# Spatial-bias buffer allocated and cleared in the opening step; ORDER and WAYS tables replaced

## The chip, the cores and the metric

The kernel runs on one core of one Trainium2 chip. The metric is device time in microseconds (us) of one execution. A core has TensorE (PE, with its weight loads shown as PEld), VectorE (DVE), ScalarE (ACT) and GpSimd (POOL). SyncE (SP) issues DMAs here and computes nothing. ACT and POOL issue DMAs as well. Each engine takes its instructions strictly in the order in which the program emits them.

## The reference, cut to what matters

Three blocks follow one another: block-causal attention, a mixture of four attention experts with two chosen per token, and a gated MLP with a spatial mix.

```python
B, H, S, D = 8, 8, 576, 64
a = softmax(mask_blocks(q @ k.T / 8)) @ v                # block-causal, blocks of 64
x = a.transpose(0, 2, 1, 3).reshape(B, S, 512)
top2, w = gate(x @ w_gate)                               # 2 of 4 experts per token
x = sum(w_e * (causal_attention(x @ wq[e], x @ wk[e], x @ wv[e]) @ wo[e]) for e in top2)
h = relu(x @ w_in)                                       # 512 -> 1024
u, v = h[..., :512], h[..., 512:]
v_s = w_spatial @ layernorm(v) + b_spatial[:, None]      # mixes the 576 positions
out = (u * v_s) @ w_out
```

## The kernel before

**Work.** The kernel goes through the 8 batches. A batch has four pairs of heads of the first attention, keys (b,0) to (b,3), and two pairs of experts, keys (b,4) and (b,5). For a pair, the steps are: `lq` and `lv` load q, k and v into a `nat` tile; `mg` finds their largest magnitude; `pq` and `pv` split q, k and v into two f16 numbers each; `sc` makes scores, their maxima and exponentials in four parts; `w` (function `weights`) splits the exponentials into two f16 numbers, a cast (first piece) and a subtraction (second piece); `wt` transposes them by a DMA from SP; `av` multiplies them with v; `x` (function `halves`) normalizes and transposes the result. For a batch, the dense steps follow: `begin`, `proj`, `vproj`, `gate`, `hv`, `norm`, `gu`, `gs`, `outp`.

**Weights.** In the first 200 us the weights are prepared beside batch 0 and 1, by the `su` steps. `ldA` loads wq, wk, wv and the gate weights. `ldB` loads w_spatial in six DMAs and then the bias b_spatial in three one-row DMAs (L615). The bias lands in a part of the tile `wspb` (`t["b"]`, 576 columns) that is set to zero first by a VectorE memset (L611). That memset stands in the seventh of the nine pieces of `ldB`. `max` takes the largest magnitudes (L632), `scale` makes scales from them, then come `cons`, `split`, `wsp` (transposes of w_spatial) and `win`, `wm`, `wout`, `wf1` to `wf3` (products of wo and w_in, and w_out).

**Order.** Every step is cut into pieces of one engine each. The list `ORDER` names the step whose next piece is emitted, so it fixes the place of each piece on each engine's queue. It was written by a planner that isn't part of the kernel. The table `WAYS` says which engine does a piece that more than one could do: A is ACT, D is DVE, G is POOL, S is SP. An entry such as "w.2.0" lists the ways for pair 2, part 0, batch by batch; the last one holds for all later batches. In "AD" the first letter is the cast and the second the subtraction. The planner's costs (`sua("ldB", ...)`, L1512) count the DMAs of `ldB`, and not the memset.

**Around the bias.** On SP, the queue in the order before runs: `ldB` pieces 1 to 6, piece 7 (the first bias DMA, after the memset), `wt` (0,0).2, `wt` (0,0).0, `ldB` 8 and 9, then `wt` (0,1).0 to 2. On DVE, the memset has 64 pieces of other steps ahead of it. On PE, `av` (0,0) comes directly ahead of the transpose of `max` (L200) and of `pq` (0,3).

Of the kernel before, what the change touches and what calls it, by code (L numbers as in the profile page):

```python
# [10 lines left out]
F32 = mybir.dt.float32  # L11
# [12 lines left out]
P = 128  # L24
# [12 lines left out]
def attn_moe_gmlp_kernel(  # L37
# [17 lines left out]
    V, A, G, T = nc.vector, nc.scalar, nc.gpsimd, nc.tensor  # L55
# [454 lines left out]
    def startup():  # L510
# [59 lines left out]
        def s_open():  # L570
            opened("su")
            TILES["x64"] = wf16.rearrange("p t c m -> p (t c m)").bitcast(U16).rearrange("p (n s) -> p n s", n=2)
# [4 lines left out]
        def s_ldA(way):  # L577
# [15 lines left out]
            t["sa"] = su.tile([P, NC], F32, name="wsa")  # L593
            V.memset(t["sa"], 0.0)

        def s_ldB(way):
# [3 lines left out]
            wb = t["wb"] = su.tile([P, 2048], F32, name="wspb")  # L600
# [9 lines left out]
            t["b"] = wb[:, 1280:1280 + S]  # L610
            V.memset(t["b"], 0.0)  # L611
# [152 lines left out]
    def dense(b, keep):  # L764
# [831 lines left out]
```

## Time and profile before

| | us |
|---|---|
| median of 3 runs | 959.12 (958.43 to 960.29) |
| the profiled execution | 963.83 |
| its span, first to last instruction | 962.10 |
| PE busy in the span | 842.6 (88%) |
| DVE busy | 734.7 (76%) |
| ACT busy | 640.0 (67%) |
| POOL busy | 533.2 (55%) |

The time of the profiled execution is 1.73 us above its span and 4.71 us above the median. The views below give busy times by stretch, waits by their releaser (the instruction whose end let the waiting one go), and the instructions in order of time. In the order of time, a bracket such as [1.73 <-DMA pT<-p] is the idle time of that engine before the instruction and what ended it.

### The profile page before, as it was taken

What the parts mean: (1) busy time and instruction counts of PE and PEld (TensorE: products, weight loads), DVE (VectorE), ACT (ScalarE), POOL (GpSimd) and SP (SyncE); (2) the same over time, 40 slices, a digit from 0 to 9 for tenths busy, and PEclk for the clock granted to TensorE, in tenths of its full rate; (3) what the DMA queues carried; (4) which work ended last, traced back from release to release, by engine and by line L of the source; (5) the groups of instructions that cost most, each with busy time, mean ns of one, the idle gap of its engine ahead of it and who ended that gap; (6) DMA issues with size and microseconds to landing.
All of it is one profiled execution on the core that took longest, in us unless ns stands there. A gap on an engine that the chain in (4) does not pass through costs nothing.

```text
span 962.1 us, 25183 instructions
## 1 busy us (share of the span) xinstructions
PE 842.6 (88%) x10038; PEld 615.3 (64%) x10038; DVE 734.7 (76%) x1602; ACT 640.0 (67%) x1159; POOL 533.2 (55%) x529
## 2 busy tenths in 40 slices
PE   3646778678999899989899999999999999999987
PEld 1444657556776677656676777666766776567654
DVE  5879979978879867887687889676898776568361
ACT  1664756987578758786577879675877767637232
POOL 6426335764673778767366667654457755516300
PEclk9777899789999999999999999999999999999999
DMA  9689988998889788999399978996799929932701
GB/s 201 161 154 213 203 164 138 179 173 142 148 161 200 126 154 149 187 184 173 75 154 214 143 145 178 160 176 121 149 172 193 153 48 160 185 70 47 157 8 55
DMA packets 472844, 143.66 MB, mean 149 GB/s; under 512 B 458307, under 2 KB 464771, under 8 KB 472726
## 3 DMA queue, kind: packets, MB, share of 16 engines
q1 hardware_dynamic: 464166, 130.31, 75.3%
q0 software_dynamic: 4944, 10.85, 4.9%
q8 instruction: 79, 1.29, 0.6%
q10 hardware_dynamic: 3616, 0.89, 0.5%
q14 instruction: 39, 0.32, 0.1%
HBM read 38.19 MB, written 9.44 MB: 50 GB/s over the span
## 4 chain that ended last, share of the span: by engine, by line
PE 53%; DVE 12%; DMA 5%; ACT 4%; issue 3%; SPq 2%; POOL 1%; DVEq 0%; ACTq 0%; POOLq 0%
PE duo L803 8%; PE duo L470 8%; PE duo L979 8%; PE duo L997 7%; PE duo L882 5%; PE duo L826 4%; PE duo L393 4%; DMA pT<-p 4%; PE duo L963 3%; DVE st L414 3%; PE duo L408 2%; ACT pf L435 2%; PE duo L345 2%; DVE qk L239 1%; DVE pf L499 1%
## 5 line engine op out<-in xcount | busy, mean ns | idle before, releaser
L455 POOL TENSOR_TENSOR p<-pf,p 128x512 f16<-128x512 f32 (+1 forms) x200 | 244.3, 1246 | 89.1 <-ACT p L352 34.1
L414 DVE TENSOR_REDUCE st<-duo 128x2 f32<-128x1024 f32 (+2 forms) x192 | 151.1, 814 | 31.2 <-PE duo L403 19.6
L470 PEld LDWEIGHTS <-pT 128*128 128x128 f16 x4320 | 143.0, 99 | 39.4 <-DMA pT<-p 21.8
L393 PE MATMUL duo<-qk 64*128 64x256 f16 (+3 forms) x1152 | 110.7, 313 | 19.7 <-DVE qk L239 11.7
L435 ACT ACTIVATE pf<-duo,st,es 128x512 f32<-128x512 f32 (+2 forms) x224 | 122.5, 615 | 8.2 <-DVE st L426 4.2
L356 POOL TENSOR_SCALAR p<-pf 128x1024 f16<-128x1024 f32 (+1 forms) x61 | 68.3, 1122 | 92.0 <-issue 26.7
L470 PE MATMUL duo<-v,pT 128*128 128x65 f16 (+1 forms) x2880 | 100.4, 195 | 20.0 <-DMA pT<-p 14.7
L979 PE MATMUL duo<-wsp,vn 128*128 128x288 f16 x832 | 111.6, 286 | 1.4 <-DVE vn L928 0.7
L803 PE MATMUL duo<-x,wqk 128*128 128x288 f16 x768 | 102.8, 294 | 6.8 <-DVE neh L218 3.9
L979 PEld LDWEIGHTS <-vn 128*128 128x128 f16 x832 | 80.1, 98 | 23.0 <-DVE vn L928 1.7
L803 PEld LDWEIGHTS <-wqk 128*128 128x128 f16 x768 | 76.3, 100 | 28.7 <-issue 6.9
L997 PE MATMUL duo<-wo,gT 128*128 128x512 f16 x384 | 85.7, 379 | 0.0
L393 PEld LDWEIGHTS <-qk 64*128 64x128 f16 x1152 | 46.4, 98 | 53.7 <-issue 36.4
L435 ACT ACTIVATE pf<-duo,st,mt 128x256 f32<-128x256 f32 (+3 forms) x128 | 69.9, 618 | 5.2 <-DVE st L426 2.5
L504 POOL TENSOR_TENSOR xh<-pf,xh 128x640 f16<-128x640 f32 x33 | 47.0, 1424 | 37.2 <-ACT xh L352 23.3
L997 PEld LDWEIGHTS <-gT 128*128 128x128 f16 x384 | 36.7, 98 | 42.7 <-DVE gT L986 0.5
L352 ACT CAST p<-pf 128x1024 f16<-128x1024 f32 (+1 forms) x59 | 62.7, 1064 | 0.7
L451 DVE TENSOR_TENSOR p<-pf,p 128x1024 f16<-128x1024 f32 (+1 forms) x44 | 57.4, 1305 | 7.3 <-POOL p L356 3.9
L470 PE MATMUL duo<-V,pT 128*128 128x65 f16 (+1 forms) x1440 | 50.3, 195 | 8.9 <-DMA pT<-p 5.5
L345 PE MATMUL duo<-ident,nat 128*128 128x128 f32 x320 | 51.3, 291 | 7.6 <-ACT pf L435 4.0
L826 PE MATMUL duo<-wvg,x 128*128 128x260 f16 x480 | 56.7, 274 | 1.3 <-ACT pf L435 0.9
L882 PE MATMUL duo<-wf,x 128*128 128x512 f16 x240 | 54.4, 379 | 0.6 <-DMA x<-xh 0.6
(273 smaller groups left out, 1681.5 us busy)
## 6 DMA issues: line engine op xcount, KB each, us to landing
out_dram<-pf SPq DMA_DIRECT2D x16, 512.0 KB, 4.4
nat<-in_q_dram SPq DMA_DIRECT2D x42, 128.0 KB, 3.1
nat<-in_k_dram SPq DMA_DIRECT2D x42, 128.0 KB, 3.3
wf<-in_moe_w_in_dram SPq DMA_DIRECT2D x8, 512.0 KB, 5.5
nat<-in_v_dram SPq DMA_DIRECT2D x32, 128.0 KB, 2.9
nat<-in_v_dram POOLq DMA_DIRECT2D x30, 128.0 KB, 5.7
nat<-in_q_dram POOLq DMA_DIRECT2D x20, 128.0 KB, 4.1
nat<-in_k_dram POOLq DMA_DIRECT2D x20, 128.0 KB, 4.6
```

The source lines that it names most:

```text
L345: T.transpose(ps[:, P * c:P * c + r], p.nat[0:r, i, c, :], ident[0:r, 0:r])
L356: G.tensor_scalar(hi, src, 1.0, 1.0, op0=OP.mult, op1=OP.mult)
L393: T.matmul(ph[:, hh, o:o + w], p.q[hs, a, ts], p.k[hs, bb, 0:w], start=i == 0, stop=False)
L414: V.reduce_max(st[:, 0, 2 * c:2 * c + 2], ph[:, :, off[c]:off[c] + P * (c + 1)], axis=AX.X)
L435: A.activation(pf[:, n * hh + off[c]:n * hh + off[c] + w], ph[:, hh, off[c]:off[c] + w], AF.Exp, bias=st[:, 1, 2 * c + hh:2 * c + hh + 1], ...
L455: G.tensor_sub(lo[:, z:z + m], src[:, z:z + m], hi[:, z:z + m])
L470: T.matmul(ps[:, hh, o:o + n], pT[:, col(t, kk):col(t, kk) + P], p.v[:, hh, kk, a:a + n], start=kk == 0 and i == 0, stop=kk == nk - 1 and ...
L803: T.matmul(ps[:, MID + a:MID + a + w], wqk16[:, l, c, 2 * n + i, :], x16[c][:, r, a:a + w], start=m == 0, stop=m == 11)
L826: T.matmul(ps[:, i, :260], x16[d][:, l, P * c:P * c + P], wvg16[:, r, d, :], start=m == 0, stop=m == 11)
L882: T.matmul(ps[:, i], h16[d][:, l, P * c:P * c + P], wf16[:, r, d, FH:], start=m == 0, stop=m == 5)
L979: T.matmul(ps[:, MID + a:MID + a + n], l, wsp16[:, r, c, a:a + n], start=i == 0, stop=i == 13)
L997: T.matmul(ps[:, i], gT[:, x, d, P * c:P * c + P], wo16[:, y, d, :], start=m == 0, stop=m == 11)
```

## The change

The step `open`, which only opened the pool of weight buffers, now also allocates `wsa` and `wspb` and clears both `wsa` (5 columns) and the bias part of `wspb` (576 columns), on VectorE. `ldA` and `ldB` no longer do so. Nothing else in the functions or in the planner's costs differs. `ORDER` and `WAYS` are replaced as a whole; the list has the same 3671 entries for the same 1366 steps.

```diff
         def s_open():
             opened("su")
+            t["sa"] = su.tile([P, NC], F32, name="wsa")
+            V.memset(t["sa"], 0.0)
+            t["wb"] = su.tile([P, 2048], F32, name="wspb")
+            t["b"] = t["wb"][:, 1280:1280 + S]
+            V.memset(t["b"], 0.0)
...
             t["st"] = su.tile([P, 5], F32, name="wst")
-            t["sa"] = su.tile([P, NC], F32, name="wsa")
-            V.memset(t["sa"], 0.0)
...
-            wb = t["wb"] = su.tile([P, 2048], F32, name="wspb")
+            wb = t["wb"]
...
-            t["b"] = wb[:, 1280:1280 + S]
-            V.memset(t["b"], 0.0)
             for i in range(3):
...
     ORDER = (
-        50, 54, 50, 54, 51, 50, 50, 50, 54, 50, 50, 52, 142, 142, 142, 143, 51, 62, 54, 143, 143, 0, 54, 143, 143,
-        54, 19, 143, 58, 58, 66, 54, 1, 58, 51, 66, 66, 56, 67, 67, 58, 58, 144, 67, 70, 1, 144, 144, 71, 62, 1, 58,
...
+        50, 54, 54, 51, 50, 50, 50, 50, 54, 50, 50, 52, 142, 142, 142, 143, 143, 51, 54, 54, 143, 54, 143, 62, 143,
+        143, 54, 66, 58, 51, 67, 56, 58, 66, 58, 58, 66, 67, 67, 144, 144, 70, 58, 70, 58, 62, 0, 58, 144, 62, 62, 1,
...
-        "lv.3": ("G", "G", "G", "S", "G", "S", "S", "G"), "mg.0.0": ("D", "D", "A", "D", "A", "A", "D", "A"),
-        "mg.1.1": ("A", "A", "D", "A", "A", "A", "A", "D"), "mg.2.0": ("D", "A", "A", "A", "A", "A", "A", "D"),
-        "mg.2.1": ("D", "D", "D", "D", "A", "D", "A", "D"), "mg.3.0": ("A", "A", "D", "D", "A", "D"),
-        "pv.1": ("A", "A", "D", "G", "A", "G", "D", "G"), "pv.2": ("A", "G", "G", "A", "D", "A", "D", "G"),
-        "w.0.2": ("GG", "DG", "DG", "GG", "GG", "DG", "GD", "AD"), "w.1.0": ("DG", "DG", "GG"),
-        "w.1.1": ("DG", "AG", "GG", "GG", "GG", "GG", "AG", "GG"), "w.1.2": ("DD", "GG", "DG", "GG", "DG", "GG"),
-        "w.2.0": ("AD", "GG", "DD", "AG", "DD", "AD", "AD", "AG"),
-        "w.2.2": ("DD", "AD", "GG", "GG", "GG", "AG", "AD", "AG"), "w.3.0": ("AD", "AG", "AD", "DD", "DG", "GG"),
...
+        "lv.3": ("G", "G", "G", "S", "S", "S", "G"), "mg.0.0": ("D", "A", "A", "D", "A"),
+        "mg.1.1": ("A", "A", "D", "A", "D", "A", "D", "A"), "mg.2.0": ("A", "A", "A", "A", "D", "A", "D", "A"),
+        "mg.2.1": ("A", "D", "D", "A", "D", "A", "D", "A"), "mg.3.0": ("A", "A", "D", "D", "A", "D", "A"),
+        "pv.1": ("A", "D", "A", "G", "G", "A", "A", "G"), "pv.2": ("A", "G", "G", "G", "G", "A"),
+        "w.1.0": ("AG", "DG", "GG", "GG", "GG", "GG", "AG", "GG"), "w.1.1": ("DG", "AG", "GG"),
+        "w.1.2": ("AD", "GG", "AG", "GG", "DG", "GG"), "w.2.0": ("GG", "GG", "AG", "GG", "AD", "AD", "GD", "GG"),
+        "w.2.2": ("GD", "AD", "GG", "AG", "AG", "AG", "DD", "GG"), "w.3.0": ("AD", "DG", "DD", "GG", "DG", "GG"),
...
```

With the step names put in for the numbers, the start of the new list reads as follows. On DVE, `open` comes after the maxima of `sc` (0,0).0, which are its 13th piece. On SP, `ldB` 1 to 4 are mixed with `ldA`; then come `ldA` 13, `win` 1, `wt` (0,0).1, `ldB` 5, `wt` (0,0).0, `ldB` 6 to 8 (with the first two bias DMAs), `wt` (0,0).2 and `ldB` 9. The load of `win` 0 is the 13th issue on SP, where it was the 8th. On ACT, the second piece of `win` 0 keeps its place ahead of the first exponentials. Of the 620 pieces on PE, 370 keep their place in PE's order, 188 move by one place, and none by more than six.

## Rows read from the trace of the kernel before

**Rows 1.** Busy time in stretches: us, then PE, PEld, DVE, ACT, POOL (x instructions), clock, DMA share, GB/s.
```profile
40.00:60.00 20.00, 6.74 (x66) 4.08 (x65) 17.13 (x36) 13.97 (x31) 6.61 (x6) 0.67 0.44 91
80.00:100.00 20.00, 14.28 (x95) 10.71 (x95) 18.81 (x30) 11.43 (x20) 11.72 (x18) 0.67 1.16 207
100.00:120.00 20.00, 15.76 (x188) 14.86 (x188) 18.82 (x36) 15.15 (x27) 8.60 (x6) 0.94 1.11 198
160.00:200.00 40.00, 27.43 (x424) 21.06 (x423) 39.09 (x78) 35.39 (x70) 29.14 (x31) 0.85 1.06 181
300.00:400.00 100.00, 93.14 (x1202) 69.37 (x1200) 79.32 (x172) 73.53 (x138) 72.83 (x71) 1.00 0.88 157
sum 962.00, PE 842.55 PEld 615.30 DVE 734.74 ACT 639.99 POOL 533.25; mean PE 44.34 PEld 32.38 DVE 38.67 ACT 33.68 POOL 28.07
```

**Rows 2.** Waits of SP's queue, whole span: waiter and releaser, total us, times, longest us.
```profile
SPq L615 <- DVE wspb L611: 15.2, 1, 15.2
```

**Rows 3.** Order of time, 34 to 65 us: start us, us, engine, line, operation [idle before <-releaser].
```profile
34.91 2.38 POOL L455 TENSOR_TENSOR p<-pf,p 128x544 f16<-128x544 f32 x2
...
35.99 0.48 SPq L608 DMA_DIRECT2D wspb<-in_moe_w_spatial_dram  x1
...
51.15 0.54 DVE L611 MEMSET wspb<- 128x576 f32 x1
...
52.13 4.56 SPq L460 DMA_TRANSPOSE pT<-p  x2
...
56.93 0.73 DVE L354 CAST p<-pf 128x1088 f16<-128x1088 f32 x1 [1.73 <-DMA pT<-p]
...
59.35 2.86 PE L470 MATMUL duo<-v,pT 128*128 128x65 f16 x49 [12.72 <-DMA pT<-p]
59.91 0.75 DVE L632 TENSOR_REDUCE wst<-wspb 128x1 f32<-128x576 f32 x1 [0.79 <-DMA wspb<-in_moe_b_spatial_dram]
...
64.49 0.17 DVE L486 TENSOR_SCALAR rr<-duo 128x10 f32<-128x10 f32 x1 [3.63 <-PE duo L470]
```

**Rows 4.** DVE's instructions by form: line, shapes, count, busy us, mean ns, idle before.
```profile
L297 DVE TENSOR_REDUCE mst<-nat 128x2 f32<-128x1280 f32 x14 | 20.7, 1477 | 6.3 <-DMA nat<-in_q_dram 3.8 <-DMA nat<-in_k_dram 2.4
L297 DVE TENSOR_REDUCE mst<-nat 128x1 f32<-128x640 f32 x15 | 11.9, 809 | 1.3 <-DMA nat<-in_v_dram 1.3
L354 DVE CAST p<-pf 128x1024 f16<-128x1024 f32 x17 | 11.6, 683 | 0.0
L354 DVE CAST p<-pf 128x1088 f16<-128x1088 f32 x7 | 5.3, 757 | 1.8 <-DMA pT<-p 1.7
L451 DVE TENSOR_TENSOR p<-pf,p 128x1024 f16<-128x1024 f32 x29 | 35.6, 1229 | 4.6 <-POOL p L356 3.9 <-ACT p L352 0.5
L426 DVE TENSOR_SCALAR st<-st,es 128x2 f32<-128x2 f32 x16 | 6.1, 382 | 0.4
```

**Rows 5.** The same view for ACT and POOL.
```profile
L295 ACT ACTIVATE junk<-nat 128x640 bf16<-128x640 f32 x53 | 38.9, 734 | 0.9
...
L455 POOL TENSOR_TENSOR p<-pf,p 128x512 f16<-128x512 f32 x134 | 164.0, 1248 | 46.9 <-DVE p L354 13.4 <-ACT p L352 11.6 <-DVE es L326 7.4
...
L356 POOL TENSOR_SCALAR p<-pf 128x1024 f16<-128x1024 f32 x40 | 45.3, 1133 | 59.7 <-ACT pf L435 25.5 <-issue 18.3 <-DVE eso L324 10.0
```

**Rows 6.** Instructions on `wspb`, L543: ns min/median/max; then the slowest in order of time.
```profile
L543 DVE SCALAR_TENSOR_TENSOR wspb<-wf,wspb x4: 691/693/1594, 87.6 to 116.3; 128x512 int32<-128x512 int32 x4
...
111.49 3.29 POOL L455 TENSOR_TENSOR p<-pf,p 128x544 f16<-128x544 f32 x2 [1.68 <-ACT p L352]
112.11 1.59 DVE L543 SCALAR_TENSOR_TENSOR wspb<-wf,wspb 128x512 int32<-128x512 int32 x1
```

**Rows 7.** Order of time at the start: the load of `win` 0 and its readers.
```profile
9.30 0.58 SPq L531 DMA_DIRECT2D wf<-in_moe_w_in_dram  x1
...
17.88 0.66 ACT L537 ACTIVATE x<-wf 128x512 f32<-128x512 f32 x1
...
24.34 1.93 ACT L435 ACTIVATE pf<-duo,st,eso 128x384 f32<-128x384 f32 x4
```

**Rows 8.** PE's waits from 200 to 950 us, the two largest: total us, times, longest.
```profile
PE duo L470 <- DMA pT<-p: 7.5, 6, 2.0
PE duo L393 <- DVE qk L239: 6.3, 8, 2.4
```

421 rows, old and new, of tables (ORDER, WAYS) are left out of this document.

## The prediction

> **What bounds the kernel now.** I read the busy times by stretch first. They split the run in two. In a stretch of the middle, 300 to 400 us, PE is busy 93.14 of 100 us: from there on PE's own work sets the pace. Ahead of 200 us it does not: from 40 to 60 us PE is busy 6.74 of 20 us, while DVE is busy 17.13; from 80 to 120 us DVE is busy 37.6 of 40 us, and from 160 to 200 us 39.09 of 40 [rows 1]. So the weights and the first batches are held by DVE, and what the change is worth is read there, from DVE's idle time and DVE's work. Over the whole span PE is idle 962 − 842.55 = 119 us [rows 1], which is the most that any order could take away.
>
> Then I read the waits of SP's queue. The first bias DMA (L615) waited 15.2 us for the memset (L611), once [rows 2]. The order of time shows it: SP issued its last w_spatial DMA at 35.99 us and was free at 36.47; DVE came to the memset only at 51.15 us, because 64 pieces of other steps lie ahead of it in its order. Behind the waiting DMA stand two transposes (L460) that went out at 52.13 us, though the POOL subtraction that made the later of their inputs ended at 34.91 + 2.38 = 37.29 us. PE, whose next work is `av` (0,0), stood idle for 12.72 us for them and started at 59.35 [rows 3].
>
> The 15.2 us are not the gain, and neither are PE's 12.72, since DVE worked on through nearly all of that time. What DVE itself lost by the wait is its idle time with a releaser behind the stalled queue: 1.73 us before a cast that needs a buffer which a transpose gives back, 0.79 us before the maximum of the bias, which had just landed, and 3.63 us before the first instruction after `av` (0,0). Together **6.15 us** [rows 3].
>
> **The change, part by part.**
>
> *The wait.* In the new order the memset is emitted after DVE's 13th piece, the maxima of the first score block, many pieces ahead of the place where SP first needs it. So the three bias DMAs find it done, and SP goes on. What is late next on SP is its own transposes: the one of `w` (0,0).2 needs data that POOL had at 37.29 us, against a queue free at 36.47 [rows 3]; a wait of about 1 us takes the place of 15.2. What is late next on DVE is DVE's own work: the maximum of the bias comes after it in any case. I take the whole 6.15 us. Ends: 0, if the same three idle times return with another releaser, and 6.15.
>
> *The memset itself* costs 0.54 us on DVE [rows 3] and is moved, not removed. It lay in a stretch where DVE was nearly full and goes to one that it shares with the first maxima. Zero; ends −0.6 to +0.6. The clearing of five columns that is moved with it is less than a tenth of a us of these.
>
> *The table: what DVE loses up to the step `begin` of batch 0.* Comparing the entries of the two tables for the pieces that both lists emit before it: `mg` (0,2) and (1,0), first parts, go to ACT, 2 × 1.477; `mg` (0,2), second part, 0.809; the casts of `w` (0,1).0 at 0.683 and of `w` (0,1).2 and `w` (0,2).2 at 0.757 each go to ACT and POOL; the subtraction of `w` (0,2).0 goes to POOL, 1.229 [rows 4]. Sum 7.19 us. To DVE come, net, two small instructions of `sc` at 0.382 and one cast of `pv` (1,1), which I price like the cast at 0.683: 1.45 us [rows 4]. So DVE has 5.74 us less to do. It is worth this only where DVE has no idle time: 80 to 120 and 160 to 200 us, 80 of the 160 us after 40 [rows 1]. I take half, **2.9 us**; ends 0 and 5.74. ACT gets three magnitudes in five instructions at 0.734 and two casts; in 40 to 60 us it was busy 13.97 of 20 [rows 1, 5], so I price that at nothing. If that cover is gone it costs what ACT gains, near 4 us.
>
> At this point a rule of the Trainium skill speaks against the new table. The trace first: four equal instructions of L543 took 0.69 us, and 1.59 us in the one case that ran beside POOL's subtraction, which itself took 3.29 us for two halves where two others of the same shape took 2.38 [rows 3, 6]. The Trainium skill, "SBUF — State Buffer", section "Who interferes with whom", says that VectorE and GpSimd share one pair of ports and that the later one blocks fully where a VectorE instruction has two SBUF inputs and the other reads SBUF. By it, each of the three pieces that POOL takes over in pair 2 here (both of `w` (0,2).0, the cast of `w` (0,2).2) would hold DVE for up to 1.59 − 0.69 = 0.90 us, 2.7 us in all, and the table's 2.9 would be 0.2. The trace agrees with the rule in this one pair of rows; how often the pairs will meet in the new order it cannot show.
>
> *The order at the start.* The load of `win` 0 becomes SP's 13th issue, where it was the 8th. It was issued at 9.30 us and read by ACT at 17.88, and the first exponentials behind it on ACT began at 24.34 [rows 7]. A load takes at most 17.88 − 9.30 = 8.6 us by these rows. Five issues later at 0.6 us (the row's own 0.58) is 12.3 us and lands by 20.9, ahead of 24.34: free. If the five issues take three times that, it lands at 26.9 and costs ACT 2.6 us. I take 1 us; ends 0 and 2.6.
>
> *The order later.* PE's order is nearly the same: 370 of 620 pieces keep their place and 188 move by one. So a gain made ahead of 200 us moves all later work forward. But each engine's queue is laid anew, and which small waits fall away or appear can't be told from the tables. PE's two largest waits after 200 us, 7.5 and 6.3 us in total [rows 8], bound it: half of these 13.8 us, about 7 us, either way. I take 0.
>
> *Sum.* −6.15 − 2.9 + 1 = −8.05 us. Against the profiled execution's own time, 963.83, this gives 955.8. The median of the runs is 4.71 below that execution, so I forecast 959.12 − 8.05 = **951 us**.
>
> **The rivals.**
>
> *The gain does not last (same).* DVE's idle time of 6.15 us returns elsewhere, and the lighter table is taken up by ACT or by DVE's clashes with POOL. For it: the DMA share is 1.16 and 1.11 in 80 to 120 us [rows 1], so transfers already stand in line there and earlier issues may only wait longer. Against it: the share is 0.44 in 40 to 60 us [rows 1], which is where the stalled transposes will now run. Time 959, chance 0.11.
>
> *POOL becomes the last link (slower).* Up to the outputs of batch 0 the new table gives POOL seven casts of `w` and takes one, at 1.133, and gives it two subtractions of two halves each, at 1.248 [rows 5]: 6 × 1.133 + 4 × 1.248 = 11.8 us; what it gives and takes of `pv`, `x` and `norm` nearly cancels. These pieces stand right ahead of the transposes that PE waits for. If all of it came to lie between the exponentials and `av`, the time is 951 + 11.8 = 963. It decides from the point where POOL has no idle time left in a batch. It was busy 72.83 of 100 us in its fullest stretch [rows 1], which leaves 27 us per batch for 12 in two or three batches; that speaks against it. Chance 0.12.
>
> *The new order waits more in the steady part (slower).* PE's two waits double: +13.8 − 8.05 gives 965 [rows 8]. Against it stands PE's nearly unchanged order. Chance 0.07.
>
> *The change does not do what it says.* The memset still holds SP, because DVE reaches it late. Only the table is left: 959.1 − 2.9 = 956. The new place is 13 pieces into DVE's queue, so this needs DVE to be over 10 us late at its first scores. Chance 0.04.
>
> **How the numbers follow.** The forecast, faster by 3 to 18 us, has 0.66. A measurement of this kernel can tell 0.2%, 1.9 us, from no change. Faster by more than that: 0.66 + 0.04 = 0.70; within it: 0.11; slower: 0.12 + 0.07 = 0.19. The range goes down to 951 − 7 (the later order) − 2.8 (the other half of the table), about 941, and up to 964, between the two slower cases; what is left out is about 2 in 10. The likeliest case by itself is 941 to 957.
>
> **What the changed profile would show.** The wait of L615 for the memset is gone from SP's waits, and the memset stands ahead of 24.34 us, where the first exponentials began [rows 7]. The two transposes go out before 45 us, `av` (0,0) starts before 53 us, and the 3.63 us before L486 is gone. The maximum of the bias, at 59.91 before [rows 3], comes some 5 us earlier. At 200 us the same work is reached about 8 us earlier, and from there PE is busy in the same share as before. The prediction is wrong if DVE shows new idle time between 36 and 66 us with POOL or ACT as the releaser, if PE's waits for pT after 200 us grow beyond 7.5 us by more than the gain, or if POOL is above nine tenths busy in any stretch of 100 us.

## The result, and the profile after

The changed kernel takes 941.9 us (941.2 to 945.0, four runs) beside 959.24 us: 17.3 us less, a ratio of 0.9825 with a 95% interval of 0.9801 to 0.9848. The forecast was 951 us, 8.05 less. Its direction held, and the time lies at the low end of its range, but the gain is twice what its sum gives. The profiled execution takes 941.22 us with a span of 939.5. That of the kernel before took 963.83, so the two traces are 22.6 us apart where the medians are 17.3 apart, and a place compared between them can be off by some 5 us. In after.py the same work has other line numbers: L615, L632 and L803 of before are L616, L633 and L804.

Busy times by stretch of the changed kernel (us, then PE, PEld, DVE, ACT, POOL, granted clock, DMA share, GB/s), as in [rows 1]:

```profile
40.00:60.00 20.00, 13.01 (x172) 10.07 (x172) 18.95 (x46) 17.33 (x34) 6.99 (x8) 0.81 1.05 213
80.00:100.00 20.00, 8.89 (x114) 7.59 (x113) 14.76 (x26) 15.52 (x30) 10.56 (x11) 0.66 1.13 205
160.00:200.00 40.00, 26.22 (x365) 18.86 (x365) 34.80 (x62) 31.27 (x58) 29.51 (x29) 0.69 0.96 172
300.00:400.00 100.00, 95.12 (x1265) 71.44 (x1260) 80.41 (x175) 73.77 (x137) 73.16 (x71) 1.00 0.91 163
400.00:500.00 100.00, 95.03 (x1187) 69.91 (x1186) 84.99 (x180) 74.04 (x133) 68.78 (x64) 1.00 0.90 166
```

From 40 to 60 us PE now does 13.01 us of work where it did 6.74. In the steady part, which the forecast held to be the same, PE is busier too: 95.12 for 93.14 from 300 to 400 us, and 95.03 from 400 to 500, where the same view of before shows 90.19.

Order of time around the bias, 19 to 53 us, as in [rows 3]:

```profile
19.08 0.54 DVE L576 MEMSET wspb<- 128x576 f32 x1
...
36.65 1.35 SPq L460 DMA_TRANSPOSE pT<-p  x1
38.05 1.34 SPq L611 DMA_DIRECT2D wspb<-in_moe_w_spatial_dram  x1
39.43 0.76 SPq L616 DMA_DIRECT2D wspb<-in_moe_b_spatial_dram  x2
40.30 3.53 SPq L460 DMA_TRANSPOSE pT<-p  x1
...
45.18 3.10 PE L470 MATMUL duo<-v,pT 128*128 128x65 f16 x90
...
50.52 0.74 DVE L633 TENSOR_REDUCE wst<-wspb 128x1 f32<-128x576 f32 x1
...
52.63 0.15 DVE L486 TENSOR_SCALAR rr<-duo 128x10 f32<-128x10 f32 x1
```

The bias DMA (L616) waits for nothing. The first `av` starts at 45.18 instead of 59.35, the maximum of the bias is taken at 50.52 instead of 59.91, and neither it nor L486 has idle time ahead of it [rows 3]. At the first `hv` of batch 0 the changed kernel's trace is 13.9 us ahead (227.1 for 241.0 us), where the forecast had about 8.

The clash with POOL that the prediction weighed is there too, on other instructions than those of [rows 6]. Two of DVE's instructions that make the weights' scales take 1.13 us beside a subtraction on POOL; in e15 below they take 0.16:

```profile
55.21 2.27 POOL L455 TENSOR_TENSOR p<-pf,p 128x512 f16<-128x512 f32 x2
55.26 1.13 DVE L227 TENSOR_SCALAR inv<-new 128x5 int32<-128x5 int32 x1
...
56.38 1.13 DVE L645 TENSOR_SCALAR gAi<-new 128x2 int32<-128x2 int32 x1
```

Order of time at the start of the changed kernel, as in [rows 7]:

```profile
4.79 1.65 ACTq L261 DMA_DIRECT2D nat<-in_q_dram  x2
...
9.13 1.49 DVE L297 TENSOR_REDUCE mst<-nat 128x2 f32<-128x1280 f32 x1 [1.39 <-DMA nat<-in_k_dram]
...
13.59 1.49 DVE L297 TENSOR_REDUCE mst<-nat 128x2 f32<-128x1280 f32 x1
...
15.49 0.73 ACT L295 ACTIVATE junk<-nat 128x640 bf16<-128x640 f32 x1
...
17.77 1.23 DVE L414 TENSOR_REDUCE st<-duo 128x2 f32<-128x1024 f32 x1 [0.99 <-PE duo L403]
18.77 0.66 ACT L537 ACTIVATE x<-wf 128x512 f32<-128x512 f32 x1 [1.60 <-DMA wf<-in_moe_w_in_dram]
...
19.55 1.28 DVE L414 TENSOR_REDUCE st<-duo 128x2 f32<-128x768 f32 x2
...
21.34 1.93 ACT L435 ACTIVATE pf<-duo,st,eso 128x384 f32<-128x384 f32 x4
```

The same work in the kernel before, in order of time:

```profile
11.52 1.49 DVE L297 TENSOR_REDUCE mst<-nat 128x2 f32<-128x1280 f32 x1 [3.80 <-DMA nat<-in_q_dram]
...
17.72 1.48 DVE L297 TENSOR_REDUCE mst<-nat 128x2 f32<-128x1280 f32 x1
...
20.45 1.49 DVE L297 TENSOR_REDUCE mst<-nat 128x2 f32<-128x1280 f32 x1
...
22.53 1.29 DVE L414 TENSOR_REDUCE st<-duo 128x2 f32<-128x768 f32 x2 [0.60 <-PE duo L403]
```

Before the memset matters at all, DVE is 2.4 us ahead at its first magnitude and 4.8 us ahead at its first score maxima. Those are of different parts, though, 128x1024 here and 128x768 before. The 128x768 maxima, after which ACT's first exponentials start, come at 19.55 us instead of 22.53, and the exponentials at 21.34 instead of 24.34 [rows 7]: the lead there is 3.0 us. Two things differ. The first loads land earlier. And of three magnitudes that DVE took ahead of the first maxima, the third, (0,2), is now done by ACT from 15.49 us.

### The profile page after: what moved, and what is told of

It is laid out like the page before. It is cut to its first block, busy times and chain, and to the rows that moved or that the text cites. A ratio compares the mean times of both kernels' runs of the same rounds, so it can differ in the third digit from the quotient of the medians.

```text
span 939.5 us, 25180 instructions
## 1 busy us (share of the span) xinstructions
PE 841.8 (90%) x10038; PEld 615.7 (66%) x10038; DVE 748.4 (80%) x1613; ACT 634.8 (68%) x1155; POOL 544.9 (58%) x538
## 3 DMA queue, kind: packets, MB, share of 16 engines
q8 instruction: 79, 1.29, 0.6%
## 5 line engine op out<-in xcount | busy, mean ns | idle before, releaser
L470 PEld LDWEIGHTS <-pT 128*128 128x128 f16 x4320 | 146.2, 99 | 24.5 <-issue 11.7
L356 POOL TENSOR_SCALAR p<-pf 128x1024 f16<-128x1024 f32 (+1 forms) x70 | 81.2, 1161 | 95.9 <-ACT pf L435 54.2
L435 ACT ACTIVATE pf<-duo,st,es 128x512 f32<-128x512 f32 (+3 forms) x224 | 122.4, 618 | 13.3 <-DVE st L426 9.3
L393 PE MATMUL duo<-qk 64*128 64x128 f16 (+3 forms) x1152 | 113.6, 321 | 19.5 <-DVE qk L239 10.1
L470 PE MATMUL duo<-v,pT 128*128 128x65 f16 (+1 forms) x2880 | 104.9, 198 | 11.6 <-ACT pf L435 4.4
L804 PE MATMUL duo<-x,wqk 128*128 128x288 f16 x768 | 98.4, 286 | 0.4 <-DVE nef L218 0.2
L804 PEld LDWEIGHTS <-wqk 128*128 128x128 f16 x768 | 74.3, 98 | 20.0 <-issue 0.7
L408 PE MATMUL duo<-qk 128*128 128x288 f16 x288 | 48.7, 311 | 17.1 <-ACT pf L435 7.4
L345 PE MATMUL duo<-ident,nat 128*128 128x128 f32 (+1 forms) x320 | 53.6, 300 | 6.9 <-ACT pf L435 3.1
L504 POOL TENSOR_TENSOR xh<-pf,xh 128x640 f16<-128x640 f32 x28 | 39.6, 1416 | 30.5 <-ACT xh L352 24.5
L352 ACT CAST p<-pf 128x1024 f16<-128x1024 f32 (+1 forms) x53 | 56.3, 1070 | 0.7
```

Source lines behind the costliest of these rows:

```text
L345: T.transpose(ps[:, P * c:P * c + r], p.nat[0:r, i, c, :], ident[0:r, 0:r])
L356: G.tensor_scalar(hi, src, 1.0, 1.0, op0=OP.mult, op1=OP.mult)
L393: T.matmul(ph[:, hh, o:o + w], p.q[hs, a, ts], p.k[hs, bb, 0:w], start=i == 0, stop=False)
L435: A.activation(pf[:, n * hh + off[c]:n * hh + off[c] + w], ph[:, hh, off[c]:off[c] + w], AF.Exp, bias=st[:, 1, 2 * c + hh:2 * c + hh + 1], ...
L470: T.matmul(ps[:, hh, o:o + n], pT[:, col(t, kk):col(t, kk) + P], p.v[:, hh, kk, a:a + n], start=kk == 0 and i == 0, stop=kk == nk - 1 and ...
L804: T.matmul(ps[:, MID + a:MID + a + w], wqk16[:, l, c, 2 * n + i, :], x16[c][:, r, a:a + w], start=m == 0, stop=m == 11)
```

## The experiments

Theory: the memset is worth its 6 to 7 us, and the rest comes from two terms that the forecast had at +1 and at 0, the order at the start and the order later. Rivals: the gain is the engine table's, or it is the table as a whole and no place can be named. Times are medians, each beside the kernel before as timed along with it. In the diffs names stand for the numbers of `ORDER`; name:n is the n-th piece of a step.

| kernel | median, before (us) | difference | ratio (95%) |
|---|---|---|---|
| changed kernel | 941.90, 959.24 | −17.3 | 0.9825 (0.9801–0.9848) |
| e1 memset alone | 955.49, 961.94 | −6.5 | 0.9930 (0.9906–0.9953) |
| e2 tables alone | 946.03, 961.94 | −15.9 | 0.9835 (0.9794–0.9876) |
| e3 new up to first `hv` | 946.99, 961.94 | −15.0 | 0.9847 (0.9810–0.9884) |
| e4 new from first `hv` | 954.29, 961.94 | −7.7 | 0.9924 (0.9897–0.9950) |
| e5 new start | 956.88, 960.65 | −3.8 | 0.9964 (0.9943–0.9986) |
| e6 memset, 7 engines | 957.75, 960.65 | −2.9 | 0.9977 (0.9958–0.9997) |
| e7 one load later | 960.68, 960.65 | 0.0 | 1.0000 (0.9980–1.0020) |
| e8 three pieces moved | 954.65, 960.65 | −6.0 | 0.9933 (0.9908–0.9958) |
| e9 = e1 + e5 + e8 | 946.82, 960.65 | −13.8 | 0.9864 (0.9841–0.9887) |
| e10 changed, `hsc` back | 942.18, 960.65 | −18.5 | 0.9805 (0.9784–0.9826) |
| e11 = e3 + e8 | 939.74, 960.65 | −20.9 | 0.9778 (0.9763–0.9792) |
| e12 changed, middle old | 938.22, 960.65 | −22.4 | 0.9772 (0.9747–0.9797) |
| e13 = e9 + early engines | 955.84, 961.26 | −5.4 | 0.9940 (0.9922–0.9959) |
| e14 = e9 + early order | 952.59, 961.26 | −8.7 | 0.9919 (0.9892–0.9946) |
| e15 as e6, 6 engines | 956.46, 961.26 | −4.8 | 0.9954 (0.9934–0.9974) |

**The two halves of the change.**

```diff
 e1: functions of the change, ORDER and WAYS of before
 e2: functions of before, ORDER and WAYS of the change
```

> The kernel before with its own ORDER and WAYS; only the allocation and the two clearings are moved into the opening step. Theory of the three parts (an earlier start, the wait with the lighter table, the later order): the wait alone is worth the idle time of VectorE that the prediction named, 6.15 us, so 953 us. Rival, the wait is the whole gain of the first 200 us: 13 to 14 us, so 946 us. Rival, the wait is covered by VectorE's queue: 959 us. In the trace the first av begins at 59.35 us before; the theory has it near 52.8 us, where the second half of v is ready on VectorE.

> The changed kernel's ORDER and WAYS, with the clearing left in the seventh piece of ldB as before. There it stands behind the maximum of wq and wk on VectorE, which ended at 43.08 us in the changed kernel, against a queue of SP that was free for it at 39.4 us. Theory: SP waits about 4 us in place of 15.2, the first av starts 4 us later, and of the change's gain only 1 to 4 us are lost: 943 to 946 us. Rival, the move of the clearing is what the gain rests on: 953 us or more.

e1 confirms the wait's term: 6.5 us for 6.15, by its interval between 4.5 and 9.0. Its trace bears out the mechanism: none of DVE's three idle times of [rows 3] is left, and the first `av` starts at 49.33 us. But e2 has nearly the whole gain with the memset in its old place. The halves alone are worth 6.5 and 15.9, and together not 22.4 but 17.3, a difference of 5.1 us, which is as much as the intervals of the three runs leave open. What the halves share is seen in the trace. The wait of SP's queue for the memset in e2 (total us, times, longest):

```profile
SPq L615 <- DVE wspb L611: 4.1, 1, 4.1
```

And e2 in order of time:

```profile
42.71 0.54 DVE L611 MEMSET wspb<- 128x576 f32 x1
...
44.73 2.72 PE L470 MATMUL duo<-v,pT 128*128 128x65 f16 x48
```

In the new order DVE comes to the old memset at 42.71 instead of 51.15 us. SP waits 4.1 us instead of 15.2 [rows 2], and the first `av` is as early as in the whole change. So most of the stall's price belongs to the old order.

**Early and late.** The list is cut at the first `hv` of batch 0, its 901st entry in the new order.

```diff
 e3: change up to entry 901, then ORDER and WAYS of before for what is left
 e4: before up to its first hv, then ORDER and WAYS of the change
```

> The changed kernel (order, table and clearing) up to the first hv of batch 0, about 240 us of the run before, and the order and table of before for all that is left. Theory: the early part brings 13 us and the later order the rest of the 17: 946 us. Rival, all of the gain comes from the early lead and the later order adds nothing: 942 us. Rival, the early lead is lost in the steady part: 955 us or more.

> The kernel before up to the first hv of batch 0, with its waiting bias load, and the changed kernel's order and table for all that is left. Theory: the later order by itself is worth 4 to 8 us: 951 to 955 us. Rival, it is worth nothing by itself: 959 us.

The early part gives 15.0 us, 8.5 more than the memset, and the late part 7.7 where the forecast had 0. Their sum, 22.7, is 5.4 us more than the whole change gives, and the intervals of the three runs leave 5 us open. It looks as if something in the new late order costs when it follows the new early part; e11 and e12 come back to that.

**The start.**

```diff
 e5: ORDER and engines of the change for the first 122 entries, the rest of before
 e7, in ORDER of before:
-    ... lv.(0,0):2, lq.(0,3):1, lq.(0,1):4, ... lq.(0,1):6, win.0:1
+    ... lv.(0,0):2, lq.(0,1):4, ... lq.(0,1):6, lq.(0,3):1, win.0:1
```

> The old functions (late memset) with the new order and engines for the first 122 entries of the list, then the old ones: the start alone. Theory: the new start brings the first magnitude on VectorE from 11.52 to 9.13 us and the first score maxima from 22.5 to 17.8 us, and as VectorE reaches the late memset as much earlier, the wait of the bias DMA for it stays at about 15 us but everything behind it moves with it: 4.5 us faster at the end (about 957.4 beside a before of 961.9). Rival, the forecast's own term: the start costs 1 us (963). Second rival: the gain is lost at the memset or behind it, because other work stands ahead of it: no change (962).

> The kernel before with one entry of the list moved: the first load of the pair (0,3) (SP) goes behind the sixth load of (0,1), as in the new order. Theory: DMAs issued by SP and ACT wait for the DMA that lies eight before them in the order of both; without this one load ahead, ACT's last three loads of the first pair wait for transfers that ended one place earlier, the issue of ACT's L261 goes from 6.42 to about 4.8 us and the first magnitude from 11.52 to about 9.1 us; 2.4 us faster at the end. Rival: the first magnitude moves, but the next loads are as late as before and the end does not move (0). Second rival: this is the whole gain of the start (4.5 us).

e5 gives 3.8 us, as the theory says: the forecast's term had the wrong sign. e7 isolates one cause and finds it real but not enough. In the traces the DMAs that SP and ACT issue carry eight completion semaphores by turns (numbers 101 and 103 to 109), and each waits until the one before it with its number has landed. With one foreign load less ahead, ACT's first L261 goes out at 4.66 us instead of 6.42, and the first magnitude comes at 9.33 us instead of 11.52; but of the 2.2 us only 1.4 are left at the first maxima, since the third magnitude still stands ahead of them, and none at the end (0.0, with 1.9 either way). The order of time of e7:

```profile
9.33 1.49 DVE L297 TENSOR_REDUCE mst<-nat 128x2 f32<-128x1280 f32 x1 [1.60 <-DMA nat<-in_k_dram]
...
19.03 1.49 DVE L297 TENSOR_REDUCE mst<-nat 128x2 f32<-128x1280 f32 x1
...
21.11 1.29 DVE L414 TENSOR_REDUCE st<-duo 128x2 f32<-128x768 f32 x2 [0.59 <-PE duo L403]
```

In e5 the 128x768 maxima come at 19.78 us and ACT's first exponentials at 21.59, where e7 has them at 22.91 and the kernel before at 24.34. That the magnitude on ACT is what makes the difference to e7 is argued from these rows; it was not run by itself.

**The late order: one stall.** Order of time in before, 461 us:

```profile
461.29 0.15 DVE L218 TENSOR_SCALAR neh<-duo 128x1 int32<-128x1 int32 x1
...
461.50 4.40 PE L803 MATMUL duo<-x,wqk 128*128 128x288 f16 x24 [3.89 <-DVE neh L218]
```

Busy times of before in that stretch:

```profile
455.00:465.00 10.00, 6.11 (x56) 3.89 (x54) 7.28 (x26) 2.95 (x4) 1.38 (x3) 0.83 0.97 204
```

PE's projection stands still for 3.89 us for L218, which reads a PSUM buffer. L218 is DVE's second piece of `hsc`, and stands on DVE behind maxima of the next score blocks and statistics of the norm. After the idle time the granted clock is 0.83 in this stretch, and the 24 matmuls take 4.40 us.

```diff
 e8, in ORDER of before:
-    hmax.2:4, hv.2.2:1, ... hv.2.1:1, sc.(4,2).0:1, ... hmax.2:5, hv.2.0:3,
-    ... sc.(4,2).2:1, hsc.2:1, norm0.2:2, norm0.2:3, hsc.2:2
+    hmax.2:4, hmax.2:5, hv.2.2:1, ... hv.2.1:1, hsc.2:1, sc.(4,2).0:1, ...
+    hv.2.0:3, hsc.2:2, ... sc.(4,2).2:1, norm0.2:2, norm0.2:3
```

> The kernel before with three pieces moved, the last of hmax of batch 2 (VectorE) and the first two of hsc of batch 2 (PE, then VectorE), ahead of the score block (4,2).0, where the new order has them. Theory: PE's wait of 3.89 us at L803 for the instruction L218 on neh (461.5 us), which ends only when VectorE has read a PSUM buffer that PE needs, is gone, and with it the fall of PE's granted clock to 0.83 in 455 to 465 us: some 5 us faster from the outputs of batch 2 on, and that is most of the 7.5 us that the new later order gains there. Rival: another wait takes its place (PE for the exponentials of the same score blocks) and under 1 us is left. Second rival: the whole 7.5 us.

The same two instructions in e8, in order of time:

```profile
455.28 0.16 DVE L218 TENSOR_SCALAR neh<-duo 128x1 int32<-128x1 int32 x1 [0.74 <-PE duo L211]
...
457.03 3.11 PE L803 MATMUL duo<-x,wqk 128*128 128x288 f16 x24
```

And the busy times of e8 in that stretch:

```profile
455.00:465.00 10.00, 9.36 (x162) 7.77 (x163) 8.52 (x33) 7.52 (x15) 1.22 (x3) 1.00 0.82 177
```

Three of 3671 entries give 6.0 us. The wait is gone, the clock stays at 1.00 (2.4 GHz), and the 24 matmuls take 3.11 us: 3.89 us of waiting and 1.29 of slower matmuls, 5.2 us at this place.

**Do the three causes add up?**

```diff
 e9:  e1 + e5 + e8; the rest of ORDER and WAYS of before
 e10: the change, with hsc.2:1 behind sc.(4,2).1:1, and
      sc.(4,2).1:2 and norm0.2:1 to 3 ahead of hsc.2:2
```

> The kernel before with three edits: the memset in the opening step, the new order and engines for the first 122 entries, and the three pieces of hmax and hsc of batch 2 moved ahead of the score block (4,2).0; all the rest of the old table. Theory: the three causes add up, 6.5 (the memset) + 3.8 (the start) + 6.0 (the three pieces), by the medians of their runs: 16.3 us faster than before, within 2 us of the whole change, so that the rest of the new table is worth about nothing. Rival: the start and the memset serve the same idle time of VectorE and don't add up, 12.5 us. Second rival: under 10 us, because the gains are given back before the end.

> The changed kernel with the first two pieces of hsc of batch 2 put back behind the score blocks (4,2).0 and (4,2).1, as in the old order (the maxima of (4,2).1 come ahead of the second of them). Theory: PE's wait at L804 for neh comes back, 4 to 6 us slower than the changed kernel, about 12 us faster than before. Rival: in the new order PE has other work or other waits there, and nothing changes: 17 us faster than before.

e9 gives 13.8, between the 16.3 of the plain sum and the rival's 12.5. The intervals of the four runs together leave 4.5 us either way, so whether start and memset overlap isn't settled. The traces don't settle it either: the first `hv` starts at 241.02 us in before, 233.42 in e1, 235.33 in e5 and 229.33 in e9, which is 7.6 and 5.7 and together 11.7; but e4 and e8, which have the old list up to that place, start it at 238.3 and 240.2. e10 refutes its theory: with `hsc` back behind two score blocks, the changed kernel loses nothing. So the place of `hsc` alone doesn't make the stall. In before three score blocks stand ahead of it, in e10 two. The kernel has four PSUM buffers of this kind (`duo`, L91). Three score blocks and the product of `hsc` hold all four in before; in e10 one is left for the projection. The trace of e10 fits that: L218 comes at 447.91 us, 3.5 us after the product that it reads, as in before, but L804 had started at 444.39, right behind that product. No run changes the number of blocks by itself.

**Where the new order loses.**

```diff
 e11: change up to entry 901, then before, with e8's three pieces moved
 e12: change up to entry 901, before up to entry 1600 (outputs of batch 1), then change
```

> The changed kernel up to the first hv, then the old order and engines with the three pieces of hmax and hsc of batch 2 moved. Theory: the early part (14.7 us by its own run) and the three pieces (6.0 us) add up: 20.7 us faster than before, 3 us faster than the changed kernel, whose own order loses some 5 us to PE's waits at about 263 us (L345 for pf 2.6, L470 for pT 2.7). Rival: with the early part ahead, VectorE comes to the neh early enough in any case, or the gain is lost again, and the end is that of the early part alone, 14.7 us.

> The changed kernel with the old order and engines between the first hv and the outputs of batch 1 only. Theory: the changed kernel's waits at about 263 us are not there, and the late part's gain of 7 us (by its own run) comes on top of the early 14.7: 20 to 22 us faster than before, 3 to 4 us faster than the changed kernel. Rival: the late part gains less when it starts from the other order, and the end is that of the changed kernel, 17 us faster than before.

Both are faster than the changed kernel: 20.9 and 22.4 us faster than before, where that gains 17.3. So behind the first `hv`, e12 says ahead of the outputs of batch 1, the new order loses 3.6 to 5.1 us to the old one. e10, the changed kernel but for three moved pieces, was timed along with them and gains 18.5; beside it the loss is 2.4 to 4.0, each by some 3 us either way. PE's waits from 200 to 330 us in the changed kernel (total us, times, longest):

```profile
PE duo L470 <- DMA pT<-p: 3.2, 2, 2.7
PE duo L345 <- ACT pf L435: 3.1, 2, 2.6
```

The same view of e11, where neither of the two has that length:

```profile
PE duo L470 <- ACT pf L435: 1.1, 1, 1.1
...
PE duo L345 <- ACT pf L435: 0.7, 1, 0.7
```

**Engines or order.** What lies between e9 (13.8) and e11 (20.9) is the rest of the early table, 7.1 us. e13 and e14 split it. e6 and e15 try engines alone, beside the memset.

```diff
 e13: e9, and engines of the change for 34 more early steps
 e14: e11, with engines of before behind entry 122
 e6:  e1, and of the new WAYS:
-    mg.(0,2).0 D, mg.(0,2).1 D, mg.(1,0).0 D, w.(0,1).0 DG, w.(0,1).2 DD,
-    w.(0,2).0 AD, w.(0,2).2 DD
+    mg.(0,2).0 A, mg.(0,2).1 A, mg.(1,0).0 A, w.(0,1).0 AG, w.(0,1).2 AD,
+    w.(0,2).0 GG, w.(0,2).2 GD
 e15: e6, with w.(0,2).0 left at AD
```

> The kernel with three edits, and on top the new engines (34 choices) for the pieces of the early part behind entry 122; their order stays the old one. Theory: order and engines belong together; engines that hand work to POOL in the old order let POOL's subtraction of w (0,2).0 fall on VectorE's scale chain, where three instructions then take 1.0 to 1.1 us each in the place of 0.17, so this gains nothing or loses up to 3 us on the kernel with three edits (10 to 13 us faster than before). Rival: the engines alone are the missing 7 us (20 us faster than before).

> The kernel with three edits, and on top the new order of the early part up to the first hv; engines behind entry 122 stay the old ones. Theory: the order gives most of the missing 7 us: 17 to 20 us faster than before. Rival: without the engines VectorE has 5.74 us more to do in a stretch in which it is full, and nothing is gained on the three edits (13 us faster than before).

> The old order, the memset in the opening step, and of the new table only the engines of seven pieces: the first magnitudes of (0,2) and (1,0) and the second of (0,2) from VectorE to ACT, the casts of w (0,1).0 and (0,1).2 to ACT, w (0,2).0 and the cast of (0,2).2 to POOL. Theory, the forecast's own term: half of the 5.74 us taken from VectorE shows, 2.9 us beyond the memset's 6.7: 9.6 us faster than before. Rival: nothing beyond the memset's 6.7, since ACT and POOL hand the work on late or VectorE stands still beside POOL. Second rival: all of it, 12.4 us.

> The old order with the memset in the opening step and the new engines for six of the seven pieces of the earlier run; w (0,2).0 stays with ACT and VectorE as before. Theory: the three slow instructions of the scale chain (0.98, 1.14 and 1.13 us beside POOL's cast and subtraction) are back at 0.17, the scales come 2.4 us earlier than with the seven pieces, and of the other six pieces a part of their 4.5 us shows: 8 to 10 us faster than before. Rival: the loss was not that collision, and it stays near the seven pieces' own result, 2 to 3 us faster than before.

Neither part of the early table is worth anything without the other. The new engines in the old order lose 8.4 us on e9, more than expected, and the new order with the old engines loses 5.1, against both of its expectations; together they win 7.1. In e13's trace, that of the slowest of its ten runs, the scale chain is slow as its theory has it (L224, L227 and L645 take 0.87, 1.13 and 1.13 us) and ends 5.7 us later than in e9 (63.03 for 57.34); that this is most of the loss isn't shown. Up to 160 us e14 and e11 have done the same work on PE, about 1250 matmuls. Where e14 loses it is seen in its busy times from 180 to 200 us:

```profile
180.00:200.00 20.00, 12.13 (x113) 8.25 (x111) 9.53 (x25) 13.54 (x23) 10.70 (x9) 0.50 0.53 100
```

The same stretch of e11:

```profile
180.00:200.00 20.00, 14.19 (x233) 11.26 (x233) 13.42 (x29) 12.03 (x21) 13.08 (x11) 0.76 0.92 164
```

In e14 no engine is full, DMA share and all: each stands in its queue for another. Between 150 and 240 us POOL has one wait of 10.3 us for DVE, ACT one of 6.0 for DVE, DVE one of 5.8 for ACT. PE's clock is at 0.50 throughout (1.2 GHz), and PE gets 113 matmuls done where e11 does 233.

e6 is worse than the memset by itself (2.9 for 6.5, each by some 2 us either way). The order of time of e6 at the scale chain, in an execution of 964.76 us, 7 above its median:

```profile
59.44 1.04 POOL L356 TENSOR_SCALAR p<-pf 128x1024 f16<-128x1024 f32 x1 [6.14 <-issue]
59.52 0.98 DVE L224 TENSOR_SCALAR new<-new 128x5 int32<-128x5 int32 x1
...
60.56 2.28 POOL L455 TENSOR_TENSOR p<-pf,p 128x512 f16<-128x512 f32 x2
60.62 1.14 DVE L227 TENSOR_SCALAR inv<-new 128x5 int32<-128x5 int32 x1
...
61.74 1.13 DVE L645 TENSOR_SCALAR gAi<-new 128x2 int32<-128x2 int32 x1
```

The same chain in e15:

```profile
60.00 0.17 DVE L224 TENSOR_SCALAR new<-new 128x5 int32<-128x5 int32 x1
...
60.28 0.16 DVE L227 TENSOR_SCALAR inv<-new 128x5 int32<-128x5 int32 x1
...
60.42 0.16 DVE L645 TENSOR_SCALAR gAi<-new 128x2 int32<-128x2 int32 x1
```

Three instructions of five elements or fewer take 0.98, 1.14 and 1.13 us beside POOL's two pieces of `w` (0,2).0, and 0.16 to 0.17 without them. Each ends with the POOL instruction beside it. Two that lie between them on DVE (L226 and L644) took 0.17 and 0.15. The rule as the prediction told it, for two SBUF inputs, does not cover these, which have one. The same section of the Trainium skill, "SBUF — State Buffer", "Who interferes with whom", also says that VectorE's `tensor_scalar` can run in modes that use both pairs of ports, and that in such a mode the later of the two engines blocks for the whole instruction of the other. The three slow instructions agree with that; in which mode they ran no trace shows. e15 takes this collision away, and its trace has the chain end 2.3 us earlier (60.58 for 62.87); but the other six pieces do not show as a gain either: L224 comes at 60.00 us, and in e1 at 59.91. e15 ends at 4.8 us, in neither of its expected bands, and by the intervals it can't be told from e6 nor, strictly, from e1.

## Why the prediction was right or wrong

**The wait: right.** 6.15 us forecast, 6.5 measured alone. The signs named for it came: `av` before 53 us (45.18), transposes before 45 us (36.65 and 40.30), no idle time ahead of L486. The bias' maximum came 9.4 us earlier rather than 5, because the start's gain lies on top. In e1's trace DVE's three idle times are gone, as the term has it. What the forecast did not see is that the new tables take most of the same wait away: in e2 DVE reaches the old memset at 42.71 us, and beside the new tables the memset's place is worth 1.4 us by medians, with 4.5 either way.

**The table: the first step that failed.** It was costed as VectorE work taken away, half of 5.74 us. The same engines in the old order gave nothing (e6, e15) or lost (e13). The clash with POOL, which the prediction priced at up to 0.90 us for each of three pieces, came on two instructions of the changed kernel at 1.0 us each, and the early order and engines gained all the same. Why order and engines need each other is argued: a piece taken off a full engine helps only if the other engine's queue has it where it can be done. Of the early order and engines together 7.1 us came (e9 to e11), where this term had 2.9: the two work together, and the sum had no line for that.

**The order at the start: the second step that failed.** +1 us forecast, −3.8 measured (e5). The `win` 0 load was judged rightly: its 13th place came at 11.88 us, ACT waited 1.60 us for it, and the first exponentials still waited for DVE's maxima alone. But it was the only thing looked at. The row [3.80 <-DMA nat<-in_q_dram] and three magnitudes ahead of the first maxima stood in the trace of before, and `mg` (0,2) to ACT stood in the table comparison. It was counted there as work after 40 us, at half price, though it lay at 20 us, ahead of the maxima that the first exponentials wait for.

**The order later: the third step that failed.** 0 forecast, with 7 us either way. The term holds two effects: −6.0 by the removal of one stall in batch 2 (e8) and +3.6 to +5.1 behind the first `hv` (e11, e12), where PE's two new waits of 2.6 and 2.7 us stand; that they are the cause is argued from the traces. In the changed kernel the two partly cancel: the later order adds 17.3 − 15.0 = 2.3 us to the early part of e3, with some 4 us either way. That this is near the forecast's 0 is luck. The bound was made from PE's two largest sums of waits [rows 8]. The stall at L803 is one wait of 3.9 us, less than either sum and longer than any of the single waits in them. Sorted by the longest wait it would have been first. And a wait of that length cost 5.2 us rather than 3.9, since the clock fell behind it; so PE's idle time is not the most that an order can take away, as the prediction has it. As the later order adds so little, most of the 9 us that the forecast lacked lies ahead of the first `hv`: 15.0 measured (e3) for 8.05.

**The rivals.** POOL did not become the last link: its fullest stretch is 73.16 of 100 us. The gain lasted. The steady part waited less, not more: PE's waits for transposes after 200 us, 7.5 us before [rows 8], are 4.8. Of the signs of being wrong none came; DVE's one new idle time between 36 and 66 us, 0.7 us, is for PE. But none of these signs looks at the start or at a single wait.

**How it adds up**, by medians: 6.5 (e1), 7.3 more with start and stall (e9), 7.1 more with the rest of the early table (e11), and 3.6 lost again by the new order behind the first `hv`: 17.3. Each step behind the first compares two kernels, and carries some 3 us of uncertainty; beside e10 the last is 2.4.

## What to carry to other kernels

A schedule of order and engines is one thing: engines without their order, or the order without its engines, cost 5 to 8 us here, so a sum over moved pieces says little until one asks where each piece stands in its queue. Read PE's waits by the longest single wait as well as by the sum, and price a long one with the slower matmuls behind it. Read the first 25 us like any other stretch: the new order there was worth 3.8 us at the end (e5). But a lead at the start isn't kept by itself: that of e7, 1.4 us at the first exponentials, was 0.0 at the end, with 1.9 either way.

## What was not expected of the hardware

After 3.89 us of idle time PE ran 24 matmuls in 4.40 us that took 3.11 without it, with a granted clock of 0.83 in that stretch against 1.00. In a stretch of 20 us where PE got only 113 matmuls, waiting for other engines between them, 0.50 was granted (e14). A tiny VectorE instruction of 0.17 us took up to 1.14 us beside GpSimd, three times along one chain (e6). With eight DMA semaphores shared by SP and ACT, one load for a later pair held up the first magnitude by 2.2 us.
